# Attention followed by a gated unit: the spatial bias moved from matmuls to VectorE, relu of v to ScalarE, and the gated unit's blocks in another order

## The chip, the cores and the metric

The kernel runs on one core of one Trainium2 chip. The metric is device time in microseconds (us). The profile shows one execution on that core; its engines are named PE (TensorE matmul), PEld (TensorE weight load), DVE (VectorE), ACT (ScalarE), POOL (GpSimd) and SP (SyncE, which here only issues DMAs).

## The reference, cut to what matters

Eight batches. Each has grouped-query attention (16 query heads, 4 key and value heads, 384 positions, 64 per head) whose output, heads side by side, is the input `x` (384 by 1024) of a gated unit:

```python
h = np.maximum(x @ w_in, 0.0)                      # 1024 -> 1024
u, v = h[..., :512], h[..., 512:]
v_n = (v - mean(v)) / np.sqrt(var(v) + 1e-06)      # over the last axis
v_s = np.einsum('ts,bsd->btd', w_spatial, v_n) + b_spatial[None, :, None]
out = (u * v_s) @ w_out                            # 512 -> 1024
```

The gated unit's spatial product is held transposed in the kernel, with `d` on the partitions and the 384 positions `t` along the free dimension. The bias `b_spatial[t]` is therefore a row that is the same on every partition.

## The kernel before, in words

All matmul operands are fp16, sums are fp32 in PSUM. The order of every engine's instructions is that in which the Python code emits them: the scheduler is off (`manual_schedule`), and each engine works through its own queue strictly in that order, waiting on semaphores.

**Attention.** A batch is 18 units (`NU`), a unit being one of 6 blocks `m` and one of 3 key tiles `t`. `scores(n)` (L238) makes two matmuls of 512 columns into a two-bank PSUM tile `sc`, of which there are two; ScalarE takes the exponential of 128 by 1024 (L245) from it. From the second batch on the scores come as a pair, those of two units at every second unit: four matmuls, then two exponentials. `weigh(b, m, hh)` (L252) makes 12 small matmuls into the single PSUM tile `av`; VectorE takes a reciprocal (L262) and a multiply (L264, writing `x`), and only after that multiply may the next `weigh` write `av`. The blocks of `x` are then transposed into `xt`, by DMA from SP's queue (L284) in the steady batches.

**Gated unit.** It is a Python generator, `gated_unit(b)`, that yields after each matmul the number of columns that it streamed. The loop over units calls `run_fill(columns)` once per unit, which takes that many columns' worth of matmuls from the generator. So the gated unit of batch b is dealt out as filler between the attention instructions of batch b+1; that of the last batch has nothing beside it. Its parts, each in a tile of a pool of three PSUM banks (`ps_ck`, tag `ck`, handed out in turn):

- `pv`: v of 128 positions, 8 matmuls of 512 columns (L322); relu on VectorE (L332, tile `vr`), then bn_stats and bn_aggr (L334, L335). There are three of these.
- `rstd`, by Ln and Exp on ScalarE (L343, L344); `nmr` on VectorE (L346); three instructions on GpSimd that write the normalised `vn` (L351).
- `pu`: u transposed, four blocks of 8 matmuls of 384 columns (L369), relu on ScalarE (L377). In batch 0 it is done by position tiles instead (L303, L312).
- `psp`: the spatial product, four blocks of 3 matmuls of 384 columns (L386), each block after one bias matmul (L383); VectorE multiplies `psp` by `uT` into `gT` (L394).
- `po`: three row tiles by two halves, each 4 matmuls of 512 columns (L401); the first half is copied by VectorE, the second by ScalarE (L410), then a DMA writes the rows (L412, L414).

The bias matmul has a matrix `ones_b` as its weights, ones in rows 0 and 32, and `bias_b` as its moving operand, which holds the bias in row 0 as fp16 and the rest of it in row 32:

```python
nc.tensor.matmul(psp[:, 0:S], ones_b, bias_b, start=True, stop=False)
```

One batch of filler beside one batch of attention is called a stage here. On PE a steady stage before has this order. S(a,b) is a pair of scores, a digit pair is block m and key tile t; `av_m_h` is a weigh of 12 matmuls; a star gives the number of matmuls:

```
S(0_2,1_0) pv_0*5 av_0_0 pv_0*3 pv_1*2 S(1_1,1_2) av_0_1 pv_1*6 pv_2*3 S(2_0,2_1) av_1_0 pv_2*5
av_1_1 pu_0*6 S(2_2,3_0) pu_0*2 pu_1*4 av_2_0 pu_1*4 pu_2*2 S(3_1,3_2) av_2_1 pu_2*6 pu_3*7 S(4_0,4_1)
av_3_0 pu_3*1 psp_0*4 psp_1*1 av_3_1 psp_1*3 psp_2*3 S(4_2,5_0) psp_2*1 psp_3*4 po_0_0*1 av_4_0
po_0_0*3 po_0_1*2 S(5_1,5_2) av_4_1 po_0_1*2 po_1_0*4 po_1_1*3 S(0_0,0_1) av_5_0 po_1_1*1 po_2_0*4
av_5_1 po_2_1*4
```

At the very start `keep_warm(k)` (L471) issues k matmuls of 128 columns whose result nothing reads: 24, then 8, then 4, around the first transposes of k and q.

Of the kernel before, what the change touches and what calls it, by code (L numbers as in the profile page):

```python
# [1 line left out]

# [7 lines left out]
FP32 = mybir.dt.float32  # L10
# [7 lines left out]
def kernel(  # L18
# [125 lines left out]
    ones_b = cst.tile([P, P], FP16, name="ones_b")  # L144
    nc.gpsimd.memset(ones_b, 0.0)
    nc.gpsimd.memset(ones_b[0:1, :], 1.0)
    nc.gpsimd.memset(ones_b[32:33, :], 1.0)
    bias_b = cst.tile([P, S], FP16, name="bias_b")
    nc.gpsimd.memset(bias_b, 0.0)
# [121 lines left out]
    def x_tile(b):  # L271
        if b not in xts:
            xts[b] = att.tile([P, NT, NB, P], FP16, name=f"xt_{b}", tag="xt")
        return xts[b]
# [15 lines left out]


    def gated_unit(b):
        xt = x_tile(b)
        last = b == B - 1
        mv = small.tile([P, NT, 2], FP32, name=f"mv_{b}", tag="mv")
        v_r, v_n = [], []
        uT = moe.tile([P, NM, S], FP16, name=f"uT_{b}", tag="uT")

        def u_tile(st):
            pu = ps_ck.tile([P, NM, P], FP32, name=f"pu_{b}_{st}", tag="ck")  # L300
            for m in range(NM):
                for kt in range(NB):
                    nc.tensor.matmul(  # L303
                        pu[:, m],
                        w_in16[:, kt, m * P : (m + 1) * P],
                        xt[:, st, kt],
                        start=(kt == 0),
                        stop=(kt == NB - 1),
                    )
                    if m < NM - 1 or kt < NB - 1:  # L310
                        yield P
            nc.vector.tensor_scalar(  # L312
                uT[:, :, st * P : (st + 1) * P], pu, 0.0, None, op0=ALU.max
            )
            yield P

        for st in range(NT):
            if st == 2 and b == 0:
                yield from u_tile(0)
            pv = ps_ck.tile([P, 512], FP32, name=f"pv_{b}_{st}", tag="ck")  # L320
            for kt in range(NB):
                nc.tensor.matmul(  # L322
                    pv,
                    xt[:, st, kt],
                    w_in16[:, kt, DH:DFF],
                    start=(kt == 0),
                    stop=(kt == NB - 1),
                )
                if kt < NB - 1:
                    yield 512  # L330
            vr = moe.tile([P, DH], FP32, name=f"vr_{b}_{st}", tag="vr", bufs=4)
            nc.vector.tensor_scalar(vr, pv, 0.0, None, op0=ALU.max)  # L332
            stats = small.tile([P, 6], FP32, name=f"stats_{b}_{st}", tag="stats")
            nc.vector.bn_stats(stats, vr)  # L334
            nc.vector.bn_aggr(mv[:, st, :], stats)  # L335
            v_r.append(vr)
            yield 512
        rstd = small.tile([P, NT], FP32, name=f"rstd_{b}", tag="rstd")
        nmr = small.tile([P, NT], FP32, name=f"nmr_{b}", tag="nmr")

        def normal(part):
            if part == 0:
                nc.scalar.activation(rstd, mv[:, :, 1], AF.Ln, bias=eps_t)  # L343
                nc.scalar.activation(rstd, rstd, AF.Exp, scale=-0.5)  # L344
                return
            nc.vector.scalar_tensor_tensor(  # L346
                nmr, mv[:, :, 0], -1.0, rstd, op0=ALU.mult, op1=ALU.mult
            )
            for st in range(NT):
                vn = moe.tile([P, DH], FP16, name=f"vn_{b}_{st}", tag="vn", bufs=6)  # L350
                nc.gpsimd.tensor_scalar(  # L351
                    vn,
                    v_r[st],
                    rstd[:, st : st + 1],
                    nmr[:, st : st + 1],
                    op0=ALU.mult,
                    op1=ALU.add,
                )
                v_n.append(vn)

        if b == 0:
            normal(0)
            normal(1)
            for st in (1, 2):
                yield from u_tile(st)
        for m in range(NM if b else 0):
            pu = ps_ck.tile([P, 512], FP32, name=f"pu_{b}_{m}", tag="ck")
            for kt in range(NB):
                nc.tensor.matmul(  # L369
                    pu[:, 0:S].rearrange("p (t s) -> p t s", t=NT),  # L370
                    w_in16[:, kt, m * P : (m + 1) * P],
                    xt[:, :, kt],
                    start=(kt == 0),
                    stop=(kt == NB - 1),
                )
                yield S
            nc.scalar.activation(uT[:, m, :], pu[:, 0:S], AF.Relu)  # L377
            if m < 2:
                normal(m)
        gT = moe.tile([P, NM, S], FP16, name=f"gT_{b}", tag="gT")  # L380
        for m in range(NM):
            psp = ps_ck.tile([P, 512], FP32, name=f"psp_{b}_{m}", tag="ck")
            nc.tensor.matmul(psp[:, 0:S], ones_b, bias_b, start=True, stop=False)  # L383
            yield S
            for st in range(NT):
                nc.tensor.matmul(  # L386
                    psp[:, 0:S],
                    v_n[st][:, m * P : (m + 1) * P],
                    wsT16[:, st, :],
                    start=False,  # L390
                    stop=(st == NT - 1),
                )
                yield S
            nc.vector.tensor_tensor(gT[:, m, :], psp[:, 0:S], uT[:, m, :], ALU.mult)  # L394
        rows = out[b].rearrange("(p t) d -> p t d", t=NT)
        for tt in range(NT):
            osb = ops.tile([P, DM], FP32, name=f"osb_{b}_{tt}", tag="osb")
            for half in range(2):
                po = ps_ck.tile([P, 512], FP32, name=f"po_{b}_{tt}_{half}", tag="ck")
                for m in range(NM):  # L400
                    nc.tensor.matmul(  # L401
                        po,
                        gT[:, m, tt * P : (tt + 1) * P],
                        w_out16[:, m, half * 512 : (half + 1) * 512],
                        start=(m == 0),
                        stop=(m == NM - 1),
                    )
                    yield 512
                cols = slice(half * 512, (half + 1) * 512)
                (nc.scalar.copy if half else nc.vector.tensor_copy)(osb[:, cols], po)  # L410
                if last:
                    nc.sync.dma_start(rows[:, tt, cols], osb[:, cols])  # L412
            if not last:
                nc.sync.dma_start(rows[:, tt, :], osb)  # L414

    HV = NB * 512
    COLS = NT * HV + NM * NB * S + NM * (NT + 1) * S + NT * 2 * NM * 512
# [4 lines left out]
    b32 = cst.tile([1, S], FP32, name="b32")  # L422

    def load_b():
        pool.dma_start(b32, moe_b_spatial.rearrange("(a s) -> a s", a=1))

    def prep_spatial():
        lo32 = cst.tile([1, S], FP32, name="lo32")
        bp = b32.rearrange("a (p t) -> a t p", t=NT)
        hi = bias_b[0:1, :].rearrange("a (t p) -> a t p", t=NT)  # L430
        nc.gpsimd.tensor_copy(hi, bp)
        nc.gpsimd.tensor_tensor(lo32.rearrange("a (t p) -> a t p", t=NT), bp, hi, ALU.subtract)
        nc.gpsimd.tensor_copy(bias_b[32:33, :], lo32)
# [35 lines left out]
    def keep_warm(n):  # L469
        for _ in range(n):  # L470
            nc.tensor.matmul(warm[:, 0:P], ident16, ident16, start=True, stop=True)  # L471

    keep_warm(24)
# [3 lines left out]
    keep_warm(8)  # L477
    q_transposes(0, 0, 0, by_act, by_dve)
    keep_warm(4)
# [71 lines left out]
    fill = []  # L551
# [3 lines left out]
    def run_fill(cols):  # L555
        nonlocal owed
        owed = owed + cols if fill else 0.0
        while fill and owed > 0:
            try:
                owed -= next(fill[0])  # L560
            except StopIteration:
                fill.pop(0)

    early = 0
    for n in range(total + 6):
# [13 lines left out]
        if n == 10:  # L579
            fill.append(gated_unit(0))  # L580
        if n >= 2 * NU + 2 and (n - 2) % NU == 0 and (n - 2) // NU <= B:
            fill.append(gated_unit((n - 2) // NU - 1))
        if n < NU + 3:

            c = HV / 4 if 10 <= n < 14 else 2 * HV / 5 if 16 <= n else 0
            early += c
            run_fill(c)
        else:
            run_fill((COLS - (early if n < 2 * NU + 2 else 0)) / (NU if n >= 2 * NU + 2 else NU - 1))
    for g in fill:  # L590
        for _ in g:
            pass
# [29 lines left out]
```

## Time and profile before

| | |
|---|---|
| median of 3 runs | 255.22 us (255.01 to 255.54) |
| the profiled execution's own time | 255.16 us |
| its span, first to last instruction | 253.1 us |
| PE / ACT / DVE / POOL busy | 244.7 / 167.5 / 140.1 / 75.0 us |
| bias matmuls (L383) | 32 |
| relu of v (L332, DVE), 128 by 512 | 24, 691 ns each |
| psp times uT (L394, DVE), 128 by 384 | 32, 556 ns each |
| copy of po (L410, ACT), 128 by 512 | 24, 589 ns each |
| exponential (L245, ACT), 128 by 1024 | 144, 1022 ns each |
| granted TensorE clock | 1.000 |

A group's mean is the duration of one instruction on its engine. Matmuls are pipelined: what one costs in a stream is the distance of the starts, which is smaller than its duration in the profile. In the timeline a row gives start, busy time, engine, source line, operation, output and inputs, and a number in square brackets is how long the engine sat idle before it and what ended that.

### The profile page before, as it was taken

The numbers are of one execution on the slowest core, as the hardware profiler recorded it, in microseconds if no ns is written. First come the engines' busy times: TensorE is split into PE (matmuls) and PEld (weight loads), VectorE is DVE, ScalarE is ACT, GpSimd is POOL, SyncE is SP. The second block draws the span as 40 slices with busy tenths as digits, with TensorE's granted clock in tenths as the row PEclk, the third lists the DMA queues.
The fourth block names the chain that finished last, engine by engine and source line by source line (L and its number), as shares of the span: only waits on it lengthen the run. The fifth ranks groups of instructions, "written<-read, shape, count | busy, mean of one in ns | idle before, by whom it ended". The sixth has DMA issues, their size and how long they took to land.

```text
span 253.1 us, 5997 instructions
## 1 busy us (share of the span) xinstructions
PE 244.7 (97%) x2457; PEld 129.1 (51%) x2457; DVE 140.1 (55%) x365; ACT 167.5 (66%) x215; POOL 75.0 (30%) x118
## 2 busy tenths in 40 slices
PE   7998998999999999999999999999999999999993
PEld 6564657534455445544455445544455445554541
DVE  2455776755727465455727465455727465465541
ACT  3896566687686867777686867777686867761311
POOL 4698857721032500261033400451030000200200
PEclk9999999999999999999999999999999999999999
DMA  7999997999179952999299962999174442025006
GB/s 182 266 290 246 285 301 195 313 217 271 65 143 311 270 182 54 201 304 252 98 137 298 248 223 57 236 279 280 60 145 96 139 153 41 3 67 223 3 22 227
DMA packets 73803, 46.71 MB, mean 185 GB/s; under 512 B 48113, under 2 KB 68657, under 8 KB 73777
## 3 DMA queue, kind: packets, MB, share of 16 engines
q1 hardware_dynamic: 68688, 37.63, 59.7%
q0 software_dynamic: 4048, 8.46, 13.5%
q8 instruction: 19, 0.31, 0.5%
q10 hardware_dynamic: 1040, 0.26, 0.5%
q14 instruction: 8, 0.06, 0.1%
HBM read 25.76 MB, written 12.58 MB: 151 GB/s over the span
## 4 chain that ended last, share of the span: by engine, by line
PE 91%; DVE 4%; ACT 2%; issue 1%; POOL 0%; DVEq 0%; POOLq 0%
PE pv L322 17%; PE av L252 16%; PE po L401 15%; PE sc L238 15%; PE pu L369 15%; PE psp L386 6%; PE warm L471 3%; PE psp L383 2%; ACT aT L245 1%; PE pu L303 1%; DVE x L264 1%; PE qps L205 1%; DVE gT L394 1%; DVE stats L334 1%; PE xps L280 1%
## 5 line engine op out<-in xcount | busy, mean ns | idle before, releaser
L245 ACT ACTIVATE aT<-sc 128x1024 f16<-128x1024 f32 x144 | 139.5, 1022 | 55.8 <-PE sc L238 55.6
L252 PEld LDWEIGHTS <-aT 128*128 128x128 f16 x1152 | 43.9, 97 | 29.1 <-DVE vr L332 5.7
L262 DVE RECIPROCAL r<-av 128x4 f32<-128x4 f32 x96 | 17.1, 178 | 67.2 <-PE av L252 67.2
L351 POOL TENSOR_SCALAR vn<-vr,rstd,nmr 128x512 f16<-128x512 f32 x24 | 18.1, 767 | 117.2 <-DVE nmr L346 90.7
L252 PE MATMUL av<-v,aT 128*128 128x65 f16 x1152 | 52.1, 194 | 0.5 <-DVE x L264 0.5
L401 PE MATMUL po<-w_out,gT 128*128 128x512 f16 x192 | 47.9, 379 | 0.4 <-ACT osb L410 0.3
L322 PE MATMUL pv<-w_in,xt 128*128 128x512 f16 x192 | 47.0, 379 | 0.2 <-DVE osb L410 0.2
L238 PE MATMUL sc<-qT,kT 64*128 64x512 f16 x288 | 45.4, 385 | 0.4 <-ACT aT L245 0.2
L264 DVE TENSOR_TENSOR x<-av,r 128x256 f16<-128x256 f32 x96 | 40.7, 424 | 3.3
L369 PE MATMUL pu<-xt,w_in 128*128 128x384 f16 x224 | 41.5, 326 | 0.0
L175 POOL CAST q<-q 128x768 f16<-128x768 f32 (+1 forms) x36 | 25.2, 732 | 15.3 <-DMA q<-in_q_dram 10.0
L369 PEld LDWEIGHTS <-w_in 128*128 128x128 f16 x224 | 20.2, 98 | 13.7 <-issue 2.5
L322 PEld LDWEIGHTS <-xt 128*128 128x128 f16 x192 | 16.6, 97 | 18.0 <-issue 1.9
L401 PEld LDWEIGHTS <-gT 128*128 128x128 f16 x192 | 16.5, 97 | 16.3 <-DVE gT L394 2.2
L394 DVE TENSOR_TENSOR gT<-psp,uT 128x384 f16<-128x384 f32 x32 | 17.7, 556 | 9.9 <-PE psp L386 9.2
L238 PEld LDWEIGHTS <-kT 64*128 64x128 f16 x288 | 9.1, 94 | 26.4 <-issue 24.5
L410 ACT COPY osb<-po 128x512 f32<-128x512 f32 x24 | 14.1, 589 | 12.1 <-PE po L401 12.0
L386 PE MATMUL psp<-wsT,vn 128*128 128x384 f16 x96 | 22.0, 326 | 0.0
L332 DVE TENSOR_SCALAR vr<-pv 128x512 f32<-128x512 f32 x24 | 16.6, 691 | 9.0 <-PE pv L322 8.3
L410 DVE COPY osb<-po 128x512 f32<-128x512 f32 x24 | 16.5, 688 | 6.4 <-PE po L401 6.3
L377 ACT ACTIVATE uT<-pu 128x384 f16<-128x384 f32 x28 | 13.8, 492 | 8.4 <-PE pu L369 8.4
L334 DVE BATCH_NORM_STATS2 stats<-vr 128x6 f32<-128x512 f32 x24 | 16.7, 695 | 0.8
(55 smaller groups left out, 127.8 us busy)
## 6 DMA issues: line engine op xcount, KB each, us to landing
out_dram<-osb SPq DMA_DIRECT2D x21, 512.0 KB, 3.8
q<-in_q_dram SPq DMA_DIRECT2D x10, 768.0 KB, 6.9
q<-in_q_dram POOLq DMA_DIRECT2D x4, 768.0 KB, 10.1
v<-in_v_dram SPq DMA_DIRECT2D x6, 384.0 KB, 8.3
w_in<-in_moe_w_in_dram POOLq DMA_DIRECT2D x4, 512.0 KB, 9.7
k<-in_k_dram SPq DMA_DIRECT2D x5, 384.0 KB, 4.1
out_dram<-osb SPq DMA_DIRECT2D x6, 256.0 KB, 2.0
q<-in_q_dram SPq DMA_DIRECT2D x2, 512.0 KB, 7.0
```

The source lines that it names most:

```text
L175: f(q16s[b, j][:, lo:hi, :, hh, :], src[:, hh, lo:hi])
L238: nc.tensor.matmul(sc[:, hh], kTs[b][half, j, t * P : (t + 1) * P], qTs[b, j][half, qt], start=True, stop=True,)
L245: nc.scalar.activation(aTs[b, m][:, t], sc, AF.Exp, scale=scale)
L252: nc.tensor.matmul(av[:, i, :], aTs[b, m][:, t, hh, i * P : (i + 1) * P], v1[b % 2][:, 2 * j + hh, t, 0 : D + 1], start=(t == 0), stop=(t ...
L264: nc.vector.tensor_tensor(x16s[b][:, qt, blk : blk + 2].rearrange("p k (i d) -> p (k i) d", i=2), av[:, :, 0:D], r.to_broadcast([P, G, D]) ...
L322: nc.tensor.matmul(pv, xt[:, st, kt], w_in16[:, kt, DH:DFF], start=(kt == 0), stop=(kt == NB - 1),)
L334: nc.vector.bn_stats(stats, vr)
L369: nc.tensor.matmul(pu[:, 0:S].rearrange("p (t s) -> p t s", t=NT), w_in16[:, kt, m * P : (m + 1) * P], xt[:, :, kt], start=(kt == 0), stop ...
L386: nc.tensor.matmul(psp[:, 0:S], v_n[st][:, m * P : (m + 1) * P], wsT16[:, st, :], start=False, stop=(st == NT - 1),)
L394: nc.vector.tensor_tensor(gT[:, m, :], psp[:, 0:S], uT[:, m, :], ALU.mult)
L401: nc.tensor.matmul(po, gT[:, m, tt * P : (tt + 1) * P], w_out16[:, m, half * 512 : (half + 1) * 512], start=(m == 0), stop=(m == NM - 1),)
L410: (nc.scalar.copy if half else nc.vector.tensor_copy)(osb[:, cols], po)
```

## The change

Six things are changed.

1. The bias matmuls, `ones_b` and the fp16 pair of bias rows go. `bias_b` is now a 128 by 384 fp32 tile; the load of the bias is a DMA that repeats the row on all partitions, and GpSimd reorders it in one copy. After the three matmuls of a `psp` block VectorE makes two instructions instead of one: `g = psp + bias_b`, then `gT = g * uT`.
2. relu of v is an activation on ScalarE; bn_stats and bn_aggr stay on VectorE.
3. One generator, `stream()`, replaces the eight `gated_unit`s, and deals their blocks in another order: the first v tile of batch b+1 is done in stage b, between the last `u` block and the last `psp` block; the third row tile of `po` of batch b-1 is done in stage b; `psp` blocks lie between `pu` blocks.
4. `normal(b)` (rstd, nmr and the three `vn`) is emitted as one, in the middle of the first `u` block, where before its ScalarE part came after the first and the rest after the second `u` block.
5. The first dummy matmuls are 27, 4 and 6 instead of 24, 8 and 4.
6. The last 512 output columns of the last batch are two tiles of 256 in two banks, the first copied by ScalarE, the second by VectorE, each with its own DMA.

The order on PE in a steady stage after:

```
S(0_2,1_0) po_1_0*4 av_0_0 po_1_1*4 pv_1*1 S(1_1,1_2) av_0_1 pv_1*7 pv_2*2 S(2_0,2_1) av_1_0 pv_2*4
av_1_1 pv_2*2 pu_0*3 S(2_2,3_0) pu_0*5 pu_1*1 av_2_0 pu_1*6 S(3_1,3_2) av_2_1 pu_1*1 po_2_0*4 psp_0*3
pu_2*3 S(4_0,4_1) av_3_0 pu_2*5 psp_1*1 av_3_1 psp_1*2 pu_3*4 S(4_2,5_0) pu_3*4 psp_2*2 av_4_0 psp_2*1
pv_0*4 S(5_1,5_2) av_4_1 pv_0*4 psp_3*3 po_2_1*3 S(0_0,0_1) av_5_0 po_2_1*1 po_0_0*3 av_5_1 po_0_0*1
po_0_1*4
```

Here `po_2` is of the batch before and `pv_0` of the batch after. The other two engines' queues in the same stage, from the first shown instruction on: ScalarE has, after the exponentials of S(1_1,1_2), relu of pv_1, and relu of pv_2 after those of S(2_0,2_1); Ln and Exp of rstd and relu of pu_0 after those of S(2_2,3_0); relu of pu_1, pu_2 and pu_3 after those of S(3_1,3_2), S(4_0,4_1) and S(4_2,5_0); relu of pv_0 after those of S(5_1,5_2). VectorE has, between the two instructions of av_4_1 and those of av_5_0: bn_stats and bn_aggr of pv_0, `g` and `gT` of psp_3.

The core of the diff:

```diff
-    ones_b = cst.tile([P, P], FP16, name="ones_b")
...
-    bias_b = cst.tile([P, S], FP16, name="bias_b")
-    nc.gpsimd.memset(bias_b, 0.0)
+    bias_b = cst.tile([P, S], FP32, name="bias_b")
...
+    def v_tile(b, st):
...
+        vr = moe.tile([P, DH], FP32, name=f"vr_{b}_{st}", tag="vr", bufs=4)
+        nc.scalar.activation(vr, pv, AF.Relu)
+        stats = small.tile([P, 6], FP32, name=f"stats_{b}_{st}", tag="stats")
+        nc.vector.bn_stats(stats, vr)
+        nc.vector.bn_aggr(mvs[b][:, st, :], stats)
...
-            nc.vector.tensor_scalar(vr, pv, 0.0, None, op0=ALU.max)
...
+    def u_block(b, m):
+        pu = ps_ck.tile([P, 512], FP32, name=f"pu_{b}_{m}", tag="ck")
+        for kt in range(NB):
...
+            if m == 0 and kt == 3:
+                normal(b)
...
+        nc.scalar.activation(uT_tile(b)[:, m, :], pu[:, 0:S], AF.Relu)
...
-            nc.tensor.matmul(psp[:, 0:S], ones_b, bias_b, start=True, stop=False)
...
-            nc.vector.tensor_tensor(gT[:, m, :], psp[:, 0:S], uT[:, m, :], ALU.mult)
+    def gate(b, m):
...
+        psp = ps_ck.tile([P, 512], FP32, name=f"psp_{b}_{m}", tag="ck")
+        for st in range(NT):
+            nc.tensor.matmul(
+                psp[:, 0:S],
+                v_ns[b][st][:, m * P : (m + 1) * P],
+                wsT16[:, st, :],
+                start=(st == 0),
+                stop=(st == NT - 1),
+            )
...
+        g = moe.tile([P, S], FP32, name=f"g_{b}_{m}", tag="g")
+        nc.vector.tensor_tensor(g, psp[:, 0:S], bias_b, ALU.add)
+        nc.vector.tensor_tensor(gTs[b][:, m, :], g, uTs[b][:, m, :], ALU.mult)
...
+    def project(b, tt, half):
...
+        cuts = (512, 768, 1024) if last and tt == NT - 1 and half else (512 * half, 512 * half + 512)
+        for i, (lo, hi) in enumerate(zip(cuts, cuts[1:])):
...
+            (nc.scalar.copy if half and not i else nc.vector.tensor_copy)(
+                osb[:, lo:hi], po[:, 0 : hi - lo]
+            )
...
+    def stream():
+        for b in range(B):
+            last = b == B - 1
+            held = [project(b - 1, 2, half) for half in range(2)] if b else [(), ()]
+            ahead = () if last else v_tile(b + 1, 0)
+            if b == 0:
...
+                yield from gate(0, 0)
+                yield from islice(ahead, 4)
+                yield from gate(0, 1)
+                yield from ahead
+                yield from gate(0, 2)
+                yield from gate(0, 3)
+            else:
+                yield from v_tile(b, 1)
+                yield from v_tile(b, 2)
+                yield from u_block(b, 0)
+                yield from u_block(b, 1)
+                yield from held[0]
+                yield from gate(b, 0)
+                yield from u_block(b, 2)
+                yield from gate(b, 1)
+                yield from u_block(b, 3)
+                yield from gate(b, 2)
+                yield from ahead
+                yield from gate(b, 3)
+                yield from held[1]
+            for tt in range(NT if last else 2):
+                for half in range(2):
+                    yield from project(b, tt, half)
...
-    COLS = NT * HV + NM * NB * S + NM * (NT + 1) * S + NT * 2 * NM * 512
+    COLS = NT * HV + NM * NB * S + NM * NT * S + NT * 2 * NM * 512
...
-    keep_warm(24)
+    keep_warm(27)
...
-    keep_warm(8)
+    keep_warm(4)
...
-    keep_warm(4)
+    keep_warm(6)
...
+        elif n < 2 * NU + 4:
+            run_fill((4 * HV + NM * NT * S + 4 * NM * 512) / (NU + 4 - 3))
         else:
-            run_fill((COLS - (early if n < 2 * NU + 2 else 0)) / (NU if n >= 2 * NU + 2 else NU - 1))
+            run_fill(COLS / NU)
```

## The prediction

> **What bounds the kernel now.** I read the page first: the busy shares and the chain that ended last.
>
> ```profile
> PE 244.7 (97%) x2457; PEld 129.1 (51%) x2457; DVE 140.1 (55%) x365; ACT 167.5 (66%) x215; POOL 75.0 (30%) x118
> ...
> PE 91%; DVE 4%; ACT 2%; issue 1%; POOL 0%; DVEq 0%; POOLq 0%
> ```
>
> PE carries the chain. A busy PE is not yet a PE without waits, so the next view is the chain in order of time. Stage follows stage at a fixed distance:
>
> ```profile
> 116.73 1.19 PE pv L322 x5
> ...
> 145.20 1.19 PE pv L322 x5
> ```
>
> That is 28.47 us a stage. What its matmuls cost in a stream comes from PE's timeline of the last stage, where nothing lies between them:
>
> ```profile
> 235.78 5.36 PE L369 MATMUL pu<-xt,w_in 128*128 128x384 f16 x32
> 240.98 0.33 PE L383 MATMUL psp<-bias_b,ones_b 128*128 128x384 f16 x1
> 241.14 0.65 PE L386 MATMUL psp<-wsT,vn 128*128 128x384 f16 x3
> ...
> 243.58 5.59 PE L401 MATMUL po<-w_out,gT 128*128 128x512 f16 x24
> ```
>
> 32 matmuls of 384 columns take 240.98 - 235.78 = 5.20, 0.1625 each; a bias matmul costs the same 0.16 (240.98 to 241.14). One of 512 costs 0.216. A pair of scores costs 0.54 plus 0.10 before it, a weigh 0.38 (both from the starts of the steady timeline, 131.79, 132.33, 132.71). A stage has 9 pairs, 12 weighs, 48 matmuls of 512 and 48 of 384: 5.76 + 4.56 + 10.35 + 7.80 = 28.47. So a steady stage holds no wait worth naming: whatever leaves PE is gained whole, and any new wait is paid whole.
>
> Whether new waits arise depends on the queues of ACT and DVE; these rows price them:
>
> ```profile
> 144.59 0.61 PE L238 MATMUL sc<-qT,kT 64*128 64x512 f16 x4
> 144.70 0.58 ACT L410 COPY osb<-po 128x512 f32<-128x512 f32 x1 [0.53 <-PE po L401]
> 145.18 1.95 ACT L245 ACTIVATE aT<-sc 128x1024 f16<-128x1024 f32 x2
> 146.22 0.54 PE L252 MATMUL av<-v,aT 128*128 128x65 f16 x12
> ...
> 154.17 0.61 PE L238 MATMUL sc<-qT,kT 64*128 64x512 f16 x4
> 154.60 1.94 ACT L245 ACTIVATE aT<-sc 128x1024 f16<-128x1024 f32 x2 [1.45 <-PE sc L238]
> 156.80 0.31 ACT L343 ACTIVATE rstd<-mv,eps_t 128x3 f32<-128x3 f32 x1
> 157.14 0.21 ACT L344 ACTIVATE rstd<-rstd 128x3 f32<-128x3 f32 x1
> 157.38 0.16 DVE L346 SCALAR_TENSOR_TENSOR nmr<-mv,rstd 128x3 f32<-128x3 f32 x1 [0.46 <-ACT rstd L344]
> ```
>
> Two exponentials begin 0.43 after their pair of scores and hold ACT for 1.94; what stands behind them on ACT waits until 2.37 after the pair began. And a weigh can wait for DVE's `x`, 0.07 after it ends:
>
> ```profile
> 39.77 0.42 DVE L264 TENSOR_TENSOR x<-av,r 128x256 f16<-128x256 f32 x1
> 40.26 0.55 PE L252 MATMUL av<-v,aT 128*128 128x65 f16 x12 [0.46 <-DVE x L264]
> ```
>
> **Bias matmuls.** 32 by 0.1625 = 5.2 us leave PE, 0.65 a stage. This is the gain.
>
> **The load on DVE and ACT.** DVE loses 24 relus of 691 ns (16.6) and gains 32 instructions. `g` reads 384 fp32 of PSUM like the old multiply, 556 ns. `gT` now reads SBUF only, which no row shows for two tensors; bn_stats, which also reads SBUF, takes 695 for 512, as much as the PSUM copy (688), so I take 556, with 0.42 (`x`, 256 elements) as the lower end and bn_stats' 0.695 as the upper. That is +17.8, and DVE stays at 141. ACT gains 24 by 589 ns = 14.1 and reaches 182 of 250: busy, not a bound. All of this lies beside PE. What matters is the order.
>
> The Trainium skill, "ScalarE: Activation LUTs", section "Rules for kernel authors", gives relu to VectorE, not ScalarE; here the rows say 691 on DVE and 589 on ACT, and I go by them: the instruction gets 0.1 shorter, but it now stands behind exponentials.
>
> **First new wait: av_5_1 behind the v tile taken ahead.** Clock 0 at the pair S(5_1,5_2). PE: pair 0.54, av_4_1 to 0.92, pv_0*4 to 1.78, psp_3*3 to 2.27, po_2_1*3 to 2.92, next pair to 3.56, av_5_0 to 3.94, po*4 to 4.80; av_5_1 wants to start. ACT: exponentials to 2.37, only then relu of pv_0 to 2.88. DVE in its order: bn_stats to 3.60, bn_aggr to 3.81, `g` to 4.3, `gT` to 4.9, reciprocal and `x` of av_5_0 to 5.45. PE starts at 5.52: a wait of 0.7. `x` was ready to begin at 4.2; it waits for work queued ahead of it that itself waits for ACT.
>
> **Second: av_2_1 behind nmr.** Clock 0 at S(2_2,3_0). PE wants av_2_1 at 0.54 + 0.98 + 0.38 + 0.98 + 0.64 = 3.51. ACT has Ln and Exp behind the exponentials, to 2.84; nmr to 3.03 stands before the reciprocal and `x` of av_2_0, to 3.66. PE at 3.73: 0.2.
>
> **Third: pu_2.** It takes the bank of pu_1, whose relu on ACT lies behind the exponentials of S(3_1,3_2) (to 5.34 on the same clock, relu to 5.75). PE would be at 5.63 and goes at 5.82: 0.2. The third `vn` (3.20 + 2.27 on POOL = 5.47) is wanted at 5.46, about as late.
>
> **Fourth: av_0_0.** It needs the first exponential of S(0_2,1_0), which stands behind the copy of po_0_1, as it stood behind a copy in the rows above: pair at 144.59, weigh at 146.22, 1.63 later. There five matmuls of 512 filled the time exactly (0.54 + 1.08); now there are four (1.40): 0.2 to 0.3.
>
> **Fifth: av_1_1.** relu and statistics of pv_1 end at 4.15 on the clock of S(1_1,1_2), reciprocal and `x` at 4.76; PE wants 4.74: 0.1.
>
> Together 1.4 a stage against 0.65 gained: +0.75, in six stages +4.5.
>
> **Stage of batch 0.** There the tile ahead ends just before av_4_0, whose reciprocal stands behind its bn_stats: clock 0 at S(4_2,5_0), relu to 2.88, bn_aggr 3.81, `x` 4.44, while av_4_1 is wanted at 2.86 (pair, 3 pv, weigh, 4 matmuls of psp, pair): 1.5. Then DVE makes `g`, `gT`, the next `x`, `g`, `gT` one after another, to about 7.1, and the fourth matmul of po, which comes straight after, is wanted at 5.9: 1.2. Less 0.65: +2.0.
>
> **Last stage.** Without attention between, psp_0 follows the end of pv_2 by 16 pu and 4 po, 2.6 + 0.86 = 3.5 us, where before 32 pu covered 5.2. The chain to the third `vn` is relu 0.79, statistics to 1.72, rstd 2.30, nmr 2.50, POOL from 2.67 for 2.26: 4.94. Its matmul is wanted at 3.79: 1.2. The last `gT` comes 0.5 after po wants it, before 0.24. With the drained attention end (0.3 more) and -0.65: +1.1.
>
> **Ends of the kernel.** The dummies become 37 from 36. The chain to the first exponential goes by casts and copies; 24 dummies end at 4.34 as kps begins, so 27 would push kps to 4.67, and fewer ones behind bring q's transposes back to 5.4 (5.49 before). The first scores wait for a copy at 6.47 (6.51 before). I take 0. The timeline shows 110 ns a dummy at first and 55 from about 7.5 on; if the closed gap brings full rate before the first scores, they save 0.4, and if 27 are in the way they lose 0.3. At the end the last copy falls from 589 to some 424 ns (the `x` row has 256 elements), and a smaller last DMA may land a little sooner: -0.2. The bias's DMA lands long before stage 0's psp, its copy replaces three on POOL: nothing. SP: the last DMA transpose of x now stands behind the out of po_0_1, some 2 us later; pv_2 reads that half some 3 us after landing would be due (3.3 after issue), so nothing, with 0.5 a stage if that slack is eaten.
>
> **Sum.** 4.5 + 2.0 + 1.1 - 0.2 = +7.4 (the 5.2 is inside) on 255.16, the profiled execution's own time and within 0.1 of the median: 262.6. The walks put a gap of 0.03 to 0.04 at every step, which some neighbouring rows do not have, so I take a little off: 262.0.
>
> The Trainium skill, "SBUF — State Buffer", section "Who interferes with whom", says that a DVE instruction with two SBUF inputs contends with a GpSimd instruction that reads SBUF, and that one blocks the other whole. `gT` becomes such an instruction (the old one had one input in PSUM). No row of this trace shows it. By it the first two `gT` of a stage, which fall among POOL's `vn` and casts, could each stand behind a POOL instruction, and the sum would be a few us more.
>
> **Rivals.** Faster: the waits do not come, because ACT takes the relus between exponentials and DVE has its `x` in time; then only the bias and the end count, 255.16 - 5.2 - 0.2 = 249.8. For it speak DVE's 55% and ACT's 66%. The point from which it decides: the five waits of a stage must come to less than 0.65, that is, each chain must be 0.15 to 0.2 shorter than walked. Against it: the 1.94 of ACT is in every pair's rows and PE has no slack. Chance 0.11 (0.02 more that it ends within 0.2%).
>
> Partly hidden: only the wait behind the tile ahead, stage 0 and the last stage are real: 6 by (0.7 - 0.65) + 2.0 + 1.1 - 0.2 = +3.2, 258.4. Chance 0.22.
>
> Dearer: each chain is 0.15 longer (`gT` at its upper 0.695 instead of 0.556), five waits by six stages: +4.5, 266.5. Chance 0.15.
>
> The forecast keeps 0.5. The range reaches from 256.5 to 266.5: below it lies the faster rival, above it half of the dearer one. 0.2% is 0.5 us, about what a measurement of this kernel can tell from no change. Faster 0.11, same 0.02, slower 0.87.
>
> **What would show it.** No L383-like rows, PE's total of matmuls down by 27; stages some 29.2 us apart; PE's waits naming DVE `x` for weighs, longest once a stage between two po; in ACT's timeline relu of the tile ahead directly after two exponentials; in the last stage PE waiting for POOL's `vn`. It is wrong if stages are 27.8 apart, or if the waits are of other engines.

## The result: 263.2 us, slower by 3 %, and the profile after

| | before | after |
|---|---|---|
| median | 255.22 us | 263.19 us (263.07 to 264.08, 5 runs) |
| the profiled execution's own time, span | 255.16, 253.1 us | 263.13, 261.0 us |
| ratio to the kernel before | | 1.031, 95 % interval 1.027 to 1.035 |
| distance of steady stages | 28.47 us | 29.11 us |

In the page of after, the busy shares and the chain that ended last answer to the first two lines of the prediction:

```profile
PE 244.1 (94%) x2430; PEld 124.9 (48%) x2430; DVE 141.9 (54%) x374; ACT 181.6 (70%) x239; POOL 72.8 (28%) x112
...
PE 71%; DVE 13%; ACT 11%; issue 3%; POOLq 1%; POOL 1%; DVEq 0%; ACTq 0%
```

PE has 27 matmuls fewer (32 bias matmuls less, one dummy and four of the split last columns more). Its busy time barely falls. A matmul's record lasts longer than its distance to the next one, and the oftener a stream is broken, the less the records overlap: the 224 matmuls of `pu` have a mean of 326 ns in both pages, and cover 41.5 us before and 44.8 after. The second line says more: a fifth of the chain has passed from PE to DVE and ACT, although neither is busier than 70 %.

The chain in order of time shows the same piece of the stage 29.11 us apart, where 28.47 stood before:

```profile
93.76 1.94 PE pv L295 x9
...
122.87 1.94 PE pv L295 x9
```

The waits of PE (releaser, sum in us, times, longest) name who is late:

```profile
PE av L248 <- DVE x L260: 6.1, 8, 1.7
PE po L406 <- DVE gT L392: 1.6, 2, 1.2
PE psp L381 <- POOL vn L323: 0.8, 2, 0.4
```

Before, a weigh waited for `x` once, for 0.5. Eight waits are listed now; the longest, 1.66, is in the stage of batch 0 and not between two `po`, where the prediction put it.

A steady stage's largest wait, in rows picked from the timeline of after (start, duration, engine, operation, idle before it and what ended that):

```profile
140.72 0.61 PE L234 MATMUL sc<-qT,kT 64*128 64x512 f16 x4
141.15 1.94 ACT L241 ACTIVATE aT<-sc 128x1024 f16<-128x1024 f32 x2 [0.70 <-PE sc L234]
142.98 0.60 ACT L305 ACTIVATE vr<-pv 128x512 f32<-128x512 f32 x1
143.61 0.69 DVE L307 BATCH_NORM_STATS2 stats<-vr 128x6 f32<-128x512 f32 x1 [1.13 <-ACT vr L305]
144.34 0.18 DVE L308 BATCH_NORM_AGGREGATE mv<-stats 128x2 f32<-128x6 f32 x1
144.44 0.53 DVE L391 TENSOR_TENSOR g<-psp,bias_b 128x384 f32<-128x384 f32 x1
144.65 1.02 PE L406 MATMUL po<-w_out,gT 128*128 128x512 f16 x4
145.00 0.56 DVE L392 TENSOR_TENSOR gT<-g,uT 128x384 f16<-128x384 f32 x1
145.47 0.18 DVE L258 RECIPROCAL r<-av 128x4 f32<-128x4 f32 x1
145.69 0.42 DVE L260 TENSOR_TENSOR x<-av,r 128x256 f16<-128x256 f32 x1
146.17 0.55 PE L248 MATMUL av<-v,aT 128*128 128x65 f16 x12 [0.49 <-DVE x L260]
```

DVE is idle for 1.13 us, because bn_stats, first in its queue, waits for relu on ACT. Behind it stand bn_aggr, `g`, `gT`, and only then the reciprocal and `x` that PE needs. An engine at 54 % makes PE late by the order of its queue.

### The profile page after: what moved, and what is told of

Its sections match the earlier page's. It is cut to its first block, busy times and chain, and to the rows that moved or that the text cites. A ratio compares the mean times of both kernels' runs of the same rounds, so it can differ in the third digit from the quotient of the medians.

```text
span 261.0 us, 5982 instructions
## 1 busy us (share of the span) xinstructions
PE 244.1 (94%) x2430; PEld 124.9 (48%) x2430; DVE 141.9 (54%) x374; ACT 181.6 (70%) x239; POOL 72.8 (28%) x112
## 4 chain that ended last, share of the span: by engine, by line
PE 71%; DVE 13%; ACT 11%; issue 3%; POOLq 1%; POOL 1%; DVEq 0%; ACTq 0%
PE av L248 13%; PE pv L295 13%; PE pu L362 12%; PE sc L234 11%; PE po L406 11%; ACT aT L241 8%; PE psp L381 4%; DVE gT L392 3%; DVE x L260 3%; DVE stats L307 2%; PE warm L516 2%; DVE g L391 2%; ACT vr L305 2%; PE pu L345 1%; DVE r L258 1%
## 5 line engine op out<-in xcount | busy, mean ns | idle before, releaser
L248 PE MATMUL av<-v,aT 128*128 128x65 f16 x1152 | 53.5, 194 | 6.9 <-DVE x L260 6.1
L406 PE MATMUL po<-w_out,gT 128*128 128x512 f16 (+1 forms) x196 | 48.7, 375 | 1.9 <-DVE gT L392 1.6
L295 PE MATMUL pv<-w_in,xt 128*128 128x512 f16 x192 | 49.5, 379 | 0.0
L362 PE MATMUL pu<-xt,w_in 128*128 128x384 f16 x224 | 44.8, 326 | 0.1
L415 ACT COPY osb<-po 128x512 f32<-128x512 f32 (+1 forms) x24 | 13.9, 579 | 19.2 <-PE po L406 19.1
L415 DVE COPY osb<-po 128x512 f32<-128x512 f32 (+1 forms) x25 | 17.0, 679 | 14.8 <-PE po L406 14.8
L381 PE MATMUL psp<-wsT,vn 128*128 128x384 f16 x96 | 23.8, 326 | 0.8 <-POOL vn L323 0.8
L392 DVE TENSOR_TENSOR gT<-g,uT 128x384 f16<-128x384 f32 x32 | 19.9, 621 | 2.6
L305 ACT ACTIVATE vr<-pv 128x512 f32<-128x512 f32 x24 | 14.4, 599 | 7.3 <-PE pv L295 7.3
L391 DVE TENSOR_TENSOR g<-psp,bias_b 128x384 f32<-128x384 f32 x32 | 17.5, 546 | 2.3 <-PE psp L381 2.3
```

Of the source, the lines that this page charges most:

```text
L248: nc.tensor.matmul(av[:, i, :], aTs[b, m][:, t, hh, i * P : (i + 1) * P], v1[b % 2][:, 2 * j + hh, t, 0 : D + 1], start=(t == 0), stop=(t ...
L295: nc.tensor.matmul(pv, x_tile(b)[:, st, kt], w_in16[:, kt, DH:DFF], start=(kt == 0), stop=(kt == NB - 1),)
L362: nc.tensor.matmul(pu[:, 0:S].rearrange("p (t s) -> p t s", t=NT), w_in16[:, kt, m * P : (m + 1) * P], x_tile(b)[:, :, kt], start=(kt == 0 ...
L381: nc.tensor.matmul(psp[:, 0:S], v_ns[b][st][:, m * P : (m + 1) * P], wsT16[:, st, :], start=(st == 0), stop=(st == NT - 1),)
L391: nc.vector.tensor_tensor(g, psp[:, 0:S], bias_b, ALU.add)
L392: nc.vector.tensor_tensor(gTs[b][:, m, :], g, uTs[b][:, m, :], ALU.mult)
```

## The experiments

**The theory:** strict queues. What counts is what stands ahead of `x` and `gT` on DVE and what those instructions wait for; the bias instructions cost because they lengthen that row. **The rivals:** (a) load, the sum of work on DVE or ACT; (b) contention, a `gT` with two SBUF inputs beside GpSimd; (c) another part of the change, relu, dummies or last columns, sets the time. Runs of one group share a chip with runs of the kernel before, and each ratio is to those.

### 1. The statistics behind the next weigh's instructions

```diff
-        nc.vector.bn_stats(stats, vr)
-        nc.vector.bn_aggr(mvs[b][:, st, :], stats)
+        def statistics():
+            nc.vector.bn_stats(stats, vr)
+            nc.vector.bn_aggr(mvs[b][:, st, :], stats)
...
+        later(statistics)
```

`later` holds the two instructions back until the next weigh's reciprocal and `x` are emitted.

> The changed kernel with one thing altered: bn_stats and bn_aggr of a v tile are put on VectorE's queue after the reciprocal and multiply of the next weigh, not before them. Same instructions on every engine, same PE order. Queue theory (PE waits because the multiply that frees av stands behind statistics that wait for ScalarE): the wait of 0.66 at av_5_1 in each of six stages goes, and the 1.2 at av_4_1 in the stage of batch 0, stages become some 28.4 to 28.5 us long; about -5, 258 us. Load theory (VectorE and ScalarE simply have too much to do): the same work is there, so within 0.5 of 263.2.

259.37 us, ratio 1.015 (1.011 to 1.018). Not an instruction was saved, yet 3.8 us came back (the two executions whose granted clock stayed at 1.000 took 258.5 and 258.8 us, the two at 0.990 and 0.991 took 260.0). The stage is 28.46 (122.89 to 151.35) against 29.11. The waits of PE for `x` fall from eight to one:

```profile
PE po L422 <- DVE gT L408: 2.1, 3, 1.2
PE av L248 <- DVE x L260: 1.7, 1, 1.7
```

The load theory is out for the steady stages. The one wait left for `x`, and the longest for `gT`, are in the stage of batch 0.

### 2. No v tile taken ahead

```diff
-            ahead = () if last else v_tile(b + 1, 0)
+            ahead = ()
...
+                yield from v_tile(b, 0)
```

> The changed kernel, but the first v tile of a batch is done at the start of its own stage, not ahead in the stage before; everything else as changed. Queue theory: the long wait at av_5_1 goes (bn_stats no longer stands between psp_3's g and the multiply of av_5_0), a wait of about 0.1 like that at av_1_1 comes for the moved tile: -0.5 a stage, and -1.2 in the stage of batch 0; about -4, 259 us. Load theory: no change, 263.2 within 0.5.

261.8 us, ratio 1.023 (1.018 to 1.030; the four executions lie between 259.8 and 262.6): a miss by almost 3. The waits for `x` are down to one, but `po` now waits for `gT` five times (3.2 us, the longest 1.7), because without the tile ahead the gates stand closer together and closer to `po`: the longest is in the stage of batch 0, where all four now stand in a row. The stages are uneven, 28.74 to 29.43 us. The tile ahead carries a wait in and keeps another out.

### 3. The bias left out

This kernel leaves the addition of the bias out altogether, `g` with it.

```diff
-        nc.vector.tensor_tensor(g, psp[:, 0:S], bias_b, ALU.add)
-        nc.vector.tensor_tensor(gTs[b][:, m, :], g, uTs[b][:, m, :], ALU.mult)
+        nc.vector.tensor_tensor(gTs[b][:, m, :], psp[:, 0:S], uTs[b][:, m, :], ALU.mult)
```

> The changed kernel without the bias added at all (g left out; gT is psp times uT in one VectorE instruction, so the bias is missing from the output). It shows what the 32 added instructions cost in this order. Queue theory: 0.56 less in each chain that holds g: the wait at av_5_1 falls from 0.66 to about 0.1, the waits for gT in the stage of batch 0 and in the last stage by 1 or so; about -5, 258 us. That is still over before, although PE has 5.2 less to do, because relu behind exponentials, nmr and the v tile ahead still make waits. Rival (the added instructions are the whole loss): 250 us.

256.88 us, ratio 1.005 (1.004 to 1.007). The 32 extra instructions, 17.5 us of DVE, cost at least 6.3 us of the 263.2 (PE waits 0.5 for `qT` in this run, for the reason found in experiment 9). Even without them, and without the bias matmuls, the rest of the change is not faster than before: its stage is 28.52 us where the matmuls alone ask 27.82 (28.47 less four bias matmuls of 0.1625). So 0.6 of the 1.29 us of waits per stage belongs to the bias and 0.7 to the rest of the change.

### 4. relu of v back on VectorE

```diff
-        nc.scalar.activation(vr, pv, AF.Relu)
+        nc.vector.tensor_scalar(vr, pv, 0.0, None, op0=ALU.max)
```

> The changed kernel with relu of v back on VectorE. Queue theory: relu need not stand behind two exponentials (0.5 earlier at av_5_1) but takes 0.69 instead of 0.6 and VectorE's own time: the chain at av_5_1 is 0.2 shorter, the others within 0.1; -1 to -2, 262 us. Load theory with VectorE as the bound: 16.6 us more work on it, slower than 263.2 by some us.

262.19 us, ratio 1.026 (1.024 to 1.029); stage 29.17. DVE carries 157.7 us instead of 141.9 and the kernel is no slower. Load on DVE is not what bounds it.

### 5. `g` written back into PSUM

```diff
-        nc.vector.tensor_tensor(g, psp[:, 0:S], bias_b, ALU.add)
-        nc.vector.tensor_tensor(gTs[b][:, m, :], g, uTs[b][:, m, :], ALU.mult)
+        nc.vector.tensor_tensor(psp[:, 0:S], psp[:, 0:S], bias_b, ALU.add)
+        nc.vector.tensor_tensor(gTs[b][:, m, :], psp[:, 0:S], uTs[b][:, m, :], ALU.mult)
```

> The changed kernel, but g is written back over psp in PSUM, so that the multiply reads one operand from PSUM and one from SBUF instead of two from SBUF. Order and number of instructions as changed. Contention theory (an instruction of VectorE with two SBUF inputs is held up by GpSimd's casts: single gT of 0.71, 0.79 and 2.15 us against 0.56): every gT lasts about 0.56, the wait of 1.66 in the stage of batch 0 goes, -1.5 to -2.5, 261 us. Rival (those long gT come from something else): group mean stays at 0.62, time within 0.4 of 263.2.

261.91 us, ratio 1.025 (1.023 to 1.027). It aims at the longest wait of after, in the stage of batch 0. The timeline of after there:

```profile
46.50 2.15 DVE L392 TENSOR_TENSOR gT<-g,uT 128x384 f16<-128x384 f32 x1
46.51 0.82 POOL L160 CAST v<-v 128x768 f16<-128x768 f32 x1
...
47.28 0.95 POOL L155 CAST k<-k 128x384 f16<-128x384 f32 x2
...
49.25 0.55 PE L248 MATMUL av<-v,aT 128*128 128x65 f16 x12 [1.66 <-DVE x L260]
```

One `gT` takes 2.15 us instead of 0.56 while GpSimd casts without a pause, and `x` stands behind it. With one input in PSUM the mean of all 32 falls back from 621 to 558 ns and the wait of 1.66 is gone. Groups of the page of after, then of this run:

```profile
L392 DVE TENSOR_TENSOR gT<-g,uT 128x384 f16<-128x384 f32 x32 | 19.9, 621 | 2.6
```

```profile
L391 DVE TENSOR_TENSOR gT<-psp,uT 128x384 f16<-128x384 f32 x32 | 17.8, 558 | 1.7
```

Rival (b) is real. It is worth 1.3 us, in the stage of batch 0; the steady stage stays at 29.13. This is the rule weighed in the prediction (the Trainium skill, "SBUF — State Buffer", section "Who interferes with whom"). The runs agree with its direction. By the page the shared port pair is an exclusive lock and the order of issue decides who is blocked; here one multiply, begun at 46.50, lasted until 48.65, past three casts in a row that ended at 48.23.

### 6 and 7. The dummies alone, and the two last tiles alone, in the kernel before

```diff
-    keep_warm(24)
+    keep_warm(27)
...
-    keep_warm(8)
+    keep_warm(4)
     q_transposes(0, 0, 0, by_act, by_dve)
-    keep_warm(4)
+    keep_warm(6)
```

The second kernel makes the last 512 columns as two tiles of 256 in two banks, as the change does (`cuts`).

> The kernel before with only the dummies 27, 4, 6 instead of 24, 8, 4. Theory: PE has no gap in its first microseconds, reaches its full rate before the first scores, and the first exponential starts 0.4 to 0.6 earlier, all of which lasts to the end since ScalarE and then PE have no slack: 254.7 us. Rival (as predicted: nothing): 255.2 within 0.2.

> The kernel before with only the last 512 columns in two tiles of 256, copied by ScalarE and VectorE, each with its DMA. Theory: the last copy is 0.2 shorter and its DMA smaller: 255.0 us. Rival: the second DMA's issue waits for the first's and nothing is gained: 255.2.

255.96 us, ratio 1.001 (1.000 to 1.003), and 255.81, ratio 1.001 (1.000 to 1.002). Neither changes the time by more than the executions spread. The dummies do move the start: the first exponential begins at 6.93 us instead of 7.16. PE's timeline of run 6 shows where that is lost, in a wait that the kernel before does not have and that experiment 9 explains:

```profile
56.23 0.61 PE L238 MATMUL sc<-qT,kT 64*128 64x512 f16 x4 [0.34 <-DMA qT<-q]
```

From the start of the last copy of `po` to the end of the span it is 3.9 us before and 3.8 in run 7, whose last copy is 0.16 shorter. A gain of 0.1 can't be told from none here.

### 8. The queues rearranged

With the queue theory in hand: statistics, nmr and `vn` are emitted after the next weigh's `x`, `psp` blocks are moved off the places where two fall together, the copy of `po_0_1` goes to VectorE, and batch 0 and the last batch get orders of their own.

```diff
+        later(statistics)
...
+        later(shift)
...
-                yield from gate(b, 0)
                 yield from u_block(b, 2)
-                yield from gate(b, 1)
+                yield from gate(b, 0)
                 yield from u_block(b, 3)
+                yield from gate(b, 1)
                 yield from gate(b, 2)
                 yield from ahead
```

Here `shift` holds nmr and the three `vn`.

> A version with all parts of the change and the same matmuls, but other queues: statistics, nmr and vn are put behind the next weigh's reciprocal and multiply; blocks in the order v1 v2 u0 u1 po_2_0 u2 psp_0 u3 psp_1 psp_2, v tile ahead, psp_3, po_2_1; in batch 0 the tile ahead is spread behind psp_0 to psp_3; in the last stage psp_0 comes after u2; the second half of the first po tile is copied by VectorE, so no copy stands before the exponential that av_0_0 needs. Queue theory: nearly all waits go, stages of 27.8 to 28.0, and the 5.2 us of bias matmuls are gained after all: 250 us. Load theory: same work on VectorE and ScalarE as changed, so about 263.

254.07 us, ratio 0.994 (0.992 to 0.996): faster than both, with the instructions of the slower kernel (seven copies on another engine), but 4 short of the 250 expected. The stage is 27.9 to 28.0 us, almost the bare 27.82. Of these parts only the first was also run alone (experiment 1). Most of the 4 us is lost in one place, as the timeline and then the windows show (in those: start and end, length, busy times of PE, PEld, DVE, ACT and POOL, granted clock, DMA share, GB/s):

```profile
46.86 2.29 DVE L412 TENSOR_TENSOR gT<-g,uT 128x384 f16<-128x384 f32 x1
...
49.76 0.55 PE L248 MATMUL av<-v,aT 128*128 128x65 f16 x12 [1.80 <-DVE x L260]
```

```profile
51.00:53.00 2.00, 2.00 (x8) 0.58 (x6) 1.37 (x3) 1.54 (x2) 1.19 (x3) 0.50 1.22 226
53.00:55.00 2.00, 2.00 (x19) 1.09 (x19) 1.93 (x5) 0.40 (x1) 0.60 (x1) 0.64 1.14 97
```

The same contention, a wait of 1.80, and just behind it the granted clock at half rate for 2.00 + 1.44 = 3.4 us, which by an estimate from these rows costs 1.7 more.

### 9. The same with batch 0's sum in PSUM

```diff
-        g = moe.tile([P, S], FP32, name=f"g_{b}_{m}", tag="g")
+        g = psp[:, 0:S] if b == 0 else moe.tile([P, S], FP32, name=f"g_{b}_{m}", tag="g")
```

> The rearranged version of the run before (bias on VectorE, no bias matmuls, gates spread apart, the statistics and nmr queued behind the next weigh's recip and x), with one difference: for batch 0 alone the first instruction of a gate writes its sum back over psp in PSUM and not into the SBUF tile g. If the 2.29 us of a gT in batch 0, the wait of 1.8 us that followed, and the granted clock of 0.5 for 3.4 us behind that wait are one chain that begins with a two-input SBUF instruction beside GpSimd's casts, then gT takes about 0.56 there, the wait is under 0.5 us, the clock stays at 1.0, and the kernel takes 254.1 - 1.3 - 1.7 = about 251 us. If the wait comes from something else in batch 0 (the order of the queue, or the load of VectorE), the long wait stays and the time is 254 us again. If only the clock is a matter of chance, 252 to 253 us.

254.09 us, ratio 0.994 (0.991 to 0.996): nothing gained in the median. Yet the step itself worked: the `gT` of batch 0 take 0.56 us and the wait for `x` is gone. The next one is late. Timeline of the transfers and PE:

```profile
49.82 6.21 SPq L216 DMA_TRANSPOSE qT<-q  x2
...
56.37 0.61 PE L234 MATMUL sc<-qT,kT 64*128 64x512 f16 x4 [2.16 <-DMA qT<-q]
```

Behind that wait the granted clock is at half rate again for 3.4 us in the profiled execution. It was not in all: four of the eight had a mean granted clock of 0.991 or 0.992 and took 254.5 to 254.9 us, the other four had 0.995 to 1.000 and took 252.7 to 253.7. The scores of batch 2 want `qT`, whose transposing transfers stand in SP's queue behind the loads of batch 3. The kernel before has the same limit without a wait to show it: its `qT` is issued at 49.8 with 6.3 us to landing, 56.1, and its scores begin at 56.21. A gain on PE in the first 56 us is lost there as long as `qT` comes no earlier: 0.34 in experiment 6, 0.5 in experiment 3, 2.16 here.

### 10 and 11. The bias alone, and relu alone, in the kernel before

The first removes the bias matmul and adds `g`, and the second has `nc.scalar.activation(vr, pv, AF.Relu)`; all else is the kernel before, with its four gates in one row.

> The kernel before with one part of the change alone: the bias is added by VectorE in an instruction of its own and the bias matmuls are gone; the gates stay in their row of four, relu of v stays on VectorE, dummies and last columns are as before. Queue theory: from a gate's last psp on VectorE needs 0.55 + 0.56 = 1.1 us for a gate, 4.4 us for the four and 1.2 us for the two weighs between them, while TensorE is through with the same stretch in about 3 us, so the first po waits 2 to 3 us for the last gT in each of seven stages that have work beside them, against 0.65 us that the bias matmuls gave back: 7 x (1.4 to 2.3) is 10 to 16 us, so 265 to 271 us. That is slower than the whole change (263.2), whose dealing apart of the gates then is worth some 2 to 8 us. Theory that only TensorE's load counts: 255.2 - 5.2 = 250 us.

> The kernel before with one part of the change alone: relu of v on ScalarE (0.60 us) and not on VectorE (0.69 us); all else as before. Queue theory: ScalarE has room (66 % busy), but its relu stands behind two exponentials in the queue, so that the statistics come up to 1 us later, and v is normalised long after; nothing on the path waits for it but the last v tile's: 255.2 to 256.2 us. Theory that VectorE's load counts: 24 x 0.69 = 16.6 us less of it, which only shows if VectorE bounds a stage: 254 us or less.

The bias alone: 273.53 us, ratio 1.069 (1.066 to 1.072), above what was expected. PE waits 23 times for `gT` before `po` (12.1 us), the stage is 30.1 to 30.5 us where the clock holds, and at three places (84, 177 and 262 us) the granted clock is at half rate for some 3.4 us. At 1.7 us each, the estimate of experiment 8, these are 5.1 of the 273.5, without which the time would lie where it was expected. The chain of waits in one stage names DVE for five microseconds on end (141.0 to 146.3), from the row of gates:

```profile
143.49 0.56 DVE gT L389
144.05 0.48 DVE g L388
...
146.37 1.04 PE po L396 x4
```

relu alone: 255.64 us, ratio 1.000 (0.999 to 1.002). So of the four parts that were run alone three leave the time as it was, and the fourth costs 18 us. The other order, which the change brings along, earns 10 of those back, by the difference of 273.5 and 263.2. That is not shown alone: no run has the new order with the bias matmuls kept.

### 12. The transposing transfers ahead of the loads

```diff
-                at(w0 - NU + 11, load_q, b, 0)
...
+                at(w0 - NU + (13 if b == 3 else 11), load_q, b, 0)
```

This is against run 9; the loads of k, of the other half of q and of v are moved in the same way.

> The run before with one more difference, in SyncE's queue alone: the four loads of batch 3 (k, q, q, v, 1.5 MB) are put behind the transposing transfers of batch 2 (kT and two qT) instead of ahead of them. In the run before the gates of batch 0 no longer waited, but the scores of batch 2 waited 2.16 us for qT (until 56.37), and the granted clock was 0.55 to 0.60 behind that wait; qT was issued at 49.82, after the loads at 42.9 to 46.9, and took 6.2 us for two beside them, though q was cast by 46.9. If this queue is the bound of the first 56 us, kT is issued at about 43.9 and qT by 47, the wait is gone, and the clock stays up: 254.1 - 2.2 - 1.7 = 250.2 us, say 250 to 251. The kernel before would hide the same bound, since its first score of batch 2 came at about 56 too. If the q transfers are late for another reason (GpSimd's casts, which stand behind the normalisation of v in its queue), the wait stays at 1 to 2 us and the time at 253 to 254. If the loads of batch 3 now come too late for their casts, a new wait appears near 80 us and the time is 253 to 256.

252.82 us, ratio 0.990 (0.988 to 0.992): the fastest of all, 1.0 % under the kernel before, though not the 250 to 251 expected. The transfers and PE:

```profile
45.78 3.27 SPq L216 DMA_TRANSPOSE qT<-q  x2
49.15 0.85 SPq L80 DMA_DIRECT2D k<-in_k_dram  x1
...
54.20 4.80 SPq L280 DMA_TRANSPOSE xt<-x  x2
...
60.93 0.39 PE L306 MATMUL pv<-w_in,xt 128*128 128x512 f16 x1 [1.00 <-DMA xt<-x]
```

`qT` is issued 4 us earlier and no score waits for it. Now the transposing transfers of `x` stand behind the same loads, and PE waits 1.00 for `xt`. Steady stages are 27.9 to 28.2 us. In this profile the granted clock does not fall before PE's last matmul. Part of the rest between 252.8 and 250 lies at the end: after the last copy the span runs on for 4.3 us here and 4.2 in runs 8 and 9, against 3.3 before and 3.4 in after. Why it does is open, and the remainder was not separated further.

## Why the prediction was right, point by point

Forecast 262.0, measured 263.2. The sum by parts, by comparing the two chains at the same place of the stage. After 122.87 - 93.76 = 29.11 a steady stage is 0.64 longer. At 93.76 after stands 1.86 behind the 91.90 of before and owes nine matmuls of 512, 1.94 us, which its order does later. Together 3.8, of which one steady stage is 0.64: batch 0 lost 3.2. Six steady stages are 3.8, and 7.9 of span less 3.2 and 3.8 leave 0.9 for the last stage and the end.

| step | predicted | measured |
|---|---|---|
| stage of batch 0, start included | +2.0 | +3.2 |
| six steady stages | 6 x 0.75 = +4.5 | 6 x 0.64 = +3.8 |
| last stage and end | 1.1 - 0.2 = +0.9 | +0.9 |
| sum | +7.4 (+6.8 taken) | +7.9 |

**The waits of a steady stage.** Predicted 1.4, measured 29.11 - 27.82 = 1.29. The first, behind the tile ahead, was put at 0.7 and is 0.66 (PE is ready at 145.51, goes at 146.17; the timeline lists 0.49 as idle, since the record of the matmul ahead of it lasts until 145.67). The fourth, `av_0_0`, 0.2 to 0.3, is 0.21: that weigh lasts 0.75 and the others 0.54. The fifth, 0.1, is 0.08. The second, behind nmr, 0.2, is only 0.08. The third, 0.2, is 0.29 in the stage shown and 0.24 in later ones, from both causes that it named: the third `vn` holds PE for 0.16, and `pu_2` begins 0.05 after the relu that frees its bank has ended, 0.13 late:

```profile
133.00 0.82 PE L381 MATMUL psp<-wsT,vn 128*128 128x384 f16 x3
133.23 0.50 ACT L373 ACTIVATE uT<-pu 128x384 f16<-128x384 f32 x1
133.78 0.65 PE L362 MATMUL pu<-xt,w_in 128*128 128x384 f16 x3
```

Experiment 1 takes the waits behind the statistics away with nothing but order and gets 0.65 a stage back.

**Inside the first wait errors cancelled.** It held relu behind two exponentials for 0.6 us (ready at 1.78, begun at 2.37 on its clock, which starts at 140.72). In after the matmuls of the tile end at 142.66 and relu begins at 142.98, a delay of 0.3. But the walk gave relu 0.51 where it takes 0.60, so that its end came out at 2.88 and is 2.86: that was luck. Experiment 4 puts relu on DVE, behind no exponential, and the stage stays at 29.17: the chain is about as long with relu on either engine.

**Batch 0 was mis-sized.** The two waits it named are there, 1.20 for the weigh and 1.15 before `po`, against 1.5 and 1.2 (idle times as listed). Missing from the sum is the 1.66 of the `gT` beside casts. It was known as a possibility, priced at "a few us" outside the sum and put in the `vn` and casts of every stage. Of the 24 multiplies of the steady stages of after only three took longer than 0.56 (0.59, 0.71 and 0.79), and the stage is not shorter without them (29.13 in experiment 5); in batch 0, where the casts stand back to back, it decides. The 3.2 also holds a gain at the start that the sum had put at 0: the first exponential begins at 6.56 instead of 7.16. That the whole came within 1.2 of the forecast is in part luck, since batch 0 was put 1.2 too low and the steady stages 0.7 too high.

**The price of `gT`.** 556 was taken, with 420 to 695 as bounds; 621 is the mean, and 556 beside nothing.

**The last stage** came as told. The three matmuls of `psp_0` begin at 244.54, 245.29 and 246.03, where 0.16 apart is their stream: 1.17 lost to `vn`, where 1.2 was put. The last `gT` makes `po` 0.61 late, against 0.24 before: 0.37 more, where 0.25 was added.

**The ends.** Dummies 0 and last copy -0.2: taken alone, no change of the time for either (experiments 6 and 7).

**The rivals.** "Faster" failed at its own point: the waits are 1.29, not below 0.65. That ACT and DVE have room was true and of no use. "Partly hidden" had the right places for the large waits but left out the small ones, which make half of a stage's loss. "Dearer" asked for every chain to be 0.15 longer, by a `gT` of 0.695; most of them took 0.56.

## What to carry to other kernels

Where engines work through queues written out by hand, price a moved instruction by what stands behind it in its queue and by what it waits for, not by the share of busy time: nearly the same instructions took 263.2 us in one order and 254.1 in another. An instruction that waits for another engine belongs behind those that a busy matmul engine is about to ask for. When a stage has no slack left, look for what will be late next before counting a gain: here VectorE's row, then a transfer of q, then one of x came up one after another.

## What the runs showed of the hardware that was not expected

**Two SBUF inputs beside GpSimd.** A VectorE multiply of 128 by 384 (`gT`) took 0.56 us alone, 0.71 to 0.79 beside one or two casts in after and up to 1.22 in runs 8 and 9, 2.15 and 2.29 beside three casts back to back, and 0.56 again with one input in PSUM at the same place.

**The clock after short waits.** In runs 1, 8 and 9 a wait of PE of 1.2, 1.8 and 2.2 us in the stage of batch 0 was followed by some 3.4 us at half the granted clock. In run 10 no wait was longer than 0.9; every stage has two or three of them about 1.1 us apart, and in three of the eight a slow stretch began within 0.5 us of the last. In after, a wait of 1.66 followed by two of about 1.2 was not followed by one, nor was a wait of 1.70 in run 1, 8 us ahead of the one that was. Executions of one kernel differ in it too (experiments 1 and 9). The Trainium skill, "TensorE: Matmul & The Clock Gate", section "What's actually happening", has the clock fall after an idle window of about 3.4 us that runs free of the kernel. The length of the slow stretch agrees; the waits here were shorter than that. That the free phase decides whether a given wait is followed by a slow stretch would fit, and was not tried.
